# One score product per head and chunk from quotients of running products, with the attention run ahead of the feed-forward

## The chip, the cores and the metric

One core of one Trainium2 chip. The metric is the device time of one execution in microseconds; a kernel's figure is the median of its runs. The profile's span is some 2 us shorter than the time of the same execution.

## The reference, cut to what matters

```python
# q, k, v, alpha: (4, 8, 768, 48) float32, alpha in 0.8 .. 1
for t in range(S):
    state = alpha[:, :, t, :, None] * state + einsum('bhd,bhe->bhde', k[:, :, t], v[:, :, t])
    y[:, :, t] = einsum('bhd,bhde->bhe', q[:, :, t], state)
x = y.transpose(0, 2, 1, 3).reshape(3072, 384)
h = x @ w_in                      # w_in  (384, 2048), float64 in memory
out = (h * sigmoid(h)) @ w_out    # w_out (2048, 384), float64 in memory
```

Both halves share TensorE. The feed-forward is the same in all kernels here. The weights arrive as float64 and are turned into float32 on the chip, in 12 pieces of w_in and 16 of w_out; each piece passes through VectorE (four operations), GpSimd (three) and ScalarE (one).

## The kernel before: the parts that matter

There are 24 chunks of 128 tokens (six positions of four batch entries). The decay between tokens of a chunk is handled at seven levels: at each, eight small matmuls, a masked copy out of PSUM, and products that widen the prefix and suffix products of alpha.

```python
for L in LEVELS:                                   # 1, 2, 4 .. 64
    ps = ps_g.tile([128, 2, 512], F32, name="ps_g")
    for j in range(NP):
        for u in range(2):                         # two heads, in rows 0..47 and 64..111
            r = slice(64 * u, 64 * u + D)
            pe.matmul(ps[:, u, 64 * j : 64 * j + 64], lhsT=kp[r, j, :],
                      rhs=qp[r, j, :].rearrange(...)[:, :, 1, :], start=True, stop=True)
    dve.copy_predicated(g.rearrange(...)[:, :, :, 1, :], masks[L]..., ps[...])
    yield
    dve.tensor_tensor(x, x, two[:, :, 0:1]..., ALU.mult)      # q side
    gps.tensor_tensor(x, x, two[:, :, 1:2]..., ALU.mult)      # k side
    gps.tensor_tensor(up..., two[:, :, 0], two[:, :, 1], ALU.mult)
# ... then g @ v, q @ state, state update, transposes of the output
```

The order: all weight conversions lie beside the first four chunks. Later one chunk is in flight at a time, and its steps alternate with pieces of the feed-forward of the position before.

```python
filler, owed = weights(), 0
for ci in range(NCH):
    for pair in (chunks[0:2], chunks[2:4]) if ci == 0 else [[n] for n in chunks]:
        ...                      # a step of attention, then the filler's share
    for _ in filler: pass
    filler, owed = moe(ci), 0
```

## Time and profile before

| | before |
|---|---|
| time | 951.3 us (median; 950.65 to 952.26) |
| span of the profile | 947.5 us |
| TensorE busy | 869.3 us (92%) |
| TensorE not busy | 78.2 us, 68.5 of it in the first 165 us |
| first feed-forward matmul starts | 152.8 us |
| VectorE / GpSimd busy | 344.5 / 295.8 us |

Busy is the union of an engine's intervals. Read the rows of 40 slices for where it is low, and the table of stretches for which engine is full there. The prediction shows these lines.

### The profile page before, as it was taken

The page shows a single profiled execution, that of the slowest core. Times are in us where ns is not written, and L with a number is a line of the kernel's source. Part 1 is how long each engine was busy: PE and PEld are TensorE (multiplying, and loading weights), DVE is VectorE, ACT ScalarE, POOL GpSimd, SP SyncE. Part 2 cuts the span into 40 slices and gives each one's busy share as a digit, 9 for nine tenths or more (in the row PEclk, how much of TensorE's full clock was granted, in tenths as well). Part 3 has the DMA queues.
Part 4 walks back from the last instruction along what each step waited for, and adds up shares of the span by engine and source line. Part 5 has one row for each costly group of instructions (what it writes and reads, how often), then busy time and mean ns, then how long its engine had stood idle before and what let it go on. Part 6 is the DMA issues. An engine that isn't in the chain of part 4 may idle for free.

```text
span 947.5 us, 12698 instructions
## 1 busy us (share of the span) xinstructions
PE 869.3 (92%) x5176; PEld 564.6 (60%) x5176; DVE 344.5 (36%) x595; ACT 135.7 (14%) x242; POOL 295.8 (31%) x496
## 2 busy tenths in 40 slices
PE   5474567999999999999999999999999999999998
PEld 4473555556666556666556666556666556665454
DVE  6888987332332332332332332332232232130000
ACT  1112112121011121011121011121011111001200
POOL 6777676223222223232223232232232122020000
PEclk9996557999999999999999999999999999999999
DMA  9436224012022021022012022012022000000000
GB/s 177 93 114 135 86 89 109 1 35 34 12 42 49 1 34 33 15 43 46 4 31 34 13 42 47 5 30 35 17 42 42 1 1 1 12 15 9 0 9 25
DMA packets 107386, 36.99 MB, mean 39 GB/s; under 512 B 100673, under 2 KB 103745, under 8 KB 107329
## 3 DMA queue, kind: packets, MB, share of 16 engines
q1 hardware_dynamic: 107328, 36.19, 18.2%
q8 instruction: 41, 0.67, 0.3%
q14 instruction: 17, 0.13, 0.1%
HBM read 31.46 MB, written 4.72 MB: 38 GB/s over the span
## 4 chain that ended last, share of the span: by engine, by line
PE 81%; DVE 8%; POOL 5%; DMA 3%; issue 2%; SPq 1%; ACT 0%; POOLq 0%; ACTq 0%
PE ps_m L293 26%; PE ps_m L284 24%; PE ps_g L207 17%; PE ps_y L241 4%; DVE gt L212 3%; DMA kn<-in_k_dram 3%; PE ps_g L191 2%; PE ps_y L246 2%; PE ps_t L254 2%; PE ps_t L234 1%; DVE qp L222 1%; POOL tot L227 1%; DVE g L157 1%; POOL prod L177 1%; DVE g L152 1%
## 5 line engine op out<-in xcount | busy, mean ns | idle before, releaser
L207 PEld LDWEIGHTS ps_g<-qp,kp 48*128 48x128 f32 x2688 | 186.7, 211 | 158.0 <-issue 100.6
L284 PE MATMUL ps_m<-xt,w_in 128*128 128x512 f32 x576 | 276.8, 613 | 0.0
L293 PE MATMUL ps_m<-w_out,g 128*128 128x384 f32 x768 | 273.2, 496 | 0.0
L207 PE MATMUL ps_g<-qp,kp 48*128 48x64 f32 x2688 | 208.6, 302 | 61.7 <-DVE qp L222 57.2
L212 DVE COPY_PREDICATED gt<-mask,ps_g 128x512 f32<-128x512 uint8 x168 | 148.5, 885 | 241.7 <-PE ps_g L207 241.5
L293 PEld LDWEIGHTS ps_m<-w_out,g 128*128 128x128 f32 x768 | 137.2, 190 | 78.1 <-issue 0.5
L225 POOL TENSOR_TENSOR kp<-kp,tot 128x256 f32<-128x256 f32 x140 | 95.0, 678 | 260.2 <-PE ps_g L207 259.9
L284 PEld LDWEIGHTS ps_m<-xt,w_in 128*128 128x128 f32 x576 | 101.9, 192 | 92.9 <-issue 86.3
L287 ACT ACTIVATE g<-ps_m 128x512 f32<-128x512 f32 x96 | 57.3, 597 | 291.3 <-PE ps_m L284 291.3
L195 DVE TENSOR_TENSOR qp<-ps_g,at 128x512 f32<-128x512 f32 x24 | 16.5, 690 | 130.4 <-ACT kp L194 129.2
L222 DVE TENSOR_TENSOR qp<-qp,tot 128x256 f32<-128x256 f32 x140 | 63.4, 455 | 0.0
L241 PEld LDWEIGHTS ps_y<-vn,gt 128*128 128x128 f32 x384 | 50.0, 204 | 7.4 <-issue 4.8
L227 POOL TENSOR_TENSOR tot<-at 128x256 f32<-128x256 f32 x24 | 15.2, 632 | 120.2 <-ACT at L187 120.2
L250 DVE TENSOR_TENSOR x<-ps_y,dv 128x384 f32<-128x384 f32 x24 | 13.4, 557 | 97.4 <-PE ps_y L246 95.4
L241 PE MATMUL ps_y<-vn,gt 128*128 128x48 f32 x384 | 48.5, 282 | 0.0
L298 ACT COPY o<-ps_m 128x384 f32<-128x384 f32 x24 | 11.5, 479 | 222.5 <-PE ps_m L293 222.5
L227 POOL TENSOR_TENSOR tot<-tot 128x128 f32<-128x128 f32 (+5 forms) x140 | 36.8, 266 | 9.8
L258 POOL TENSOR_TENSOR st<-st,tot 128x384 f32<-128x384 f32 x16 | 13.2, 828 | 83.5 <-PE ps_y L246 83.5
L177 POOL TENSOR_TENSOR prod<-qn,kn 128x384 f32<-128x384 f32 x24 | 25.9, 1081 | 19.0 <-DMA kn<-in_k_dram 19.0
L159 ACT ACTIVATE g<-g 128x384 f32<-128x384 int32 (+1 forms) x28 | 15.9, 569 | 109.3 <-DVE g L157 109.3
L155 DVE SCALAR_TENSOR_TENSOR g<-bits,g 128x384 int32<-128x384 int32 (+1 forms) x28 | 22.9, 817 | 10.2 <-POOL g L154 10.2
L181 POOL TENSOR_TENSOR dv<-vn,dot 128x384 f32<-128x384 f32 x24 | 20.4, 849 | 19.3 <-DVE x L250 19.3
(51 smaller groups left out, 477.2 us busy)
## 6 DMA issues: line engine op xcount, KB each, us to landing
bits<-in_moe_w_in_dram SPq DMA_DIRECT2D x12, 512.0 KB, 4.0
bits<-in_moe_w_out_dram SPq DMA_DIRECT2D x16, 384.0 KB, 3.0
an<-in_alpha_dram SPq DMA_DIRECT2D x24, 192.0 KB, 3.1
qn<-in_q_dram SPq DMA_DIRECT2D x24, 192.0 KB, 4.0
kn<-in_k_dram SPq DMA_DIRECT2D x24, 192.0 KB, 4.1
vn<-in_v_dram SPq DMA_DIRECT2D x24, 192.0 KB, 2.5
out_dram<-o SPq DMA_DIRECT2D x24, 192.0 KB, 1.9
```

Source lines behind the costliest of these rows:

```text
L155: dve.scalar_tensor_tensor(e, hi, -(1 << 31), e, ALU.bitwise_and, ALU.bitwise_or)
L177: gps.tensor_tensor(prod, c["q"][:, :, 0:D], c["k"][:, :, 0:D], ALU.mult)
L181: gps.tensor_tensor(dv, vn, dot.to_broadcast([128, H, D]), ALU.mult)
L207: pe.matmul(ps[:, u, 64 * j : 64 * j + 64], lhsT=kp[r, j, :], rhs=qp[r, j, :].rearrange("p (b two l) -> p b two l", two=2, l=L)[:, :, 1, : ...
L212: dve.copy_predicated(g.rearrange("p u j (b two l) -> p u (j b) two l", two=2, l=L)[:, :, :, 1, :], masks[L].rearrange("p j (b l) -> p (j ...
L222: dve.tensor_tensor(x, x, two[:, :, 0:1].to_broadcast([128, nb, L]), ALU.mult)
L225: gps.tensor_tensor(x, x, two[:, :, 1:2].to_broadcast([128, nb, L]), ALU.mult)
L227: gps.tensor_tensor(up.rearrange("p j b -> p (j b)"), two[:, :, 0], two[:, :, 1], ALU.mult)
L241: pe.matmul(py[:, h, :], lhsT=g[:, h % 2, h // 2, :], rhs=vn[:, h, :], start=(h == 0), stop=(ci == 0 and h == H - 1), skip_group_check=True)
L284: pe.matmul(ps, lhsT=w_in[:, t, f * 128 : (f + 1) * 128], rhs=xt[:, t, :], start=(t == 0), stop=(t == NKT - 1))
L287: act.activation(gf, ps, AF.Silu)
L293: pe.matmul(ps, lhsT=gs[f][:, b * C : (b + 1) * C], rhs=w_out[:, f, :], start=(f == 0), stop=(f == NFT - 1))
```

## The change

The decay from s to t is a quotient of running products, P[t] / P[s]. So q is multiplied by the running product of alpha, k by a running product taken backwards that starts from one over the chunk's whole product, and one matmul per head gives all scores; a 0/1 mask then cuts off the lower half. This is exact enough only where no chunk's product gets too small. The kernel collects the largest alpha and the smallest chunk product, makes a flag of them at the end, and runs the whole old program if the flag is false.

The order changes too: the first eight chunks run ahead beside w_in alone, in four stages over consecutive steps, so four chunks are in flight. The w_out conversion moves under the first feed-forward. In the diff, which is cut, `[backwards]` stands for the reversed slices.

```diff
+    def products(n):
+        dve.tensor_reduce(most[:, n : n + 1], c["a"], ..., op=ALU.max, ...)
+        ...                                        # transposes of a, k, q; copies by ScalarE
+        dve.tensor_tensor_scan(p[...], sg[...], one[...], 0.0, ALU.mult, ALU.add)
+        dve.tensor_single_scalar(least[:, n, :], c["pc"], 2.0**-64, ALU.max)
+        dve.reciprocal(iv[:, last], least[:, n, :])
+        dve.tensor_tensor_scan(r[backwards], sg[backwards], iv[backwards], 0.0, ALU.mult, ALU.add)
+        gps.tensor_tensor(out["q"], out["q"], tokens(p), ALU.mult)
+        dve.tensor_tensor(out["k"], out["k"], tokens(r), ALU.mult)
+    def scores(n):
+        for j in range(NP):
+            for u in range(2):
+                r = slice(64 * u, 64 * u + D)
+                pe.matmul(ps[:, u, j, :], lhsT=c["kp"][r, j, :], rhs=c["qp"][r, j, :], start=True, stop=True)
+        for u in range(2):
+            dve.tensor_tensor(g[:, u], ps[:, u], mask..., ALU.mult)
+        ...                                        # transposes of k'
+    STAGES = (products, scores, values, bridge)
+    AHEAD = 2 * B
+    for step in range(steps):
+        for i, stage in enumerate(STAGES):
+            n = step - i
+            if 0 <= n < NT: stage(n)                  # ... and note in `bridged` what is ready
+            if step < AHEAD:
+                convert(0, (step * 4 + i + 1) * n_conv[0] // (4 * AHEAD))     # w_in
+            else:
+                share = todo * ((step - AHEAD) * 4 + i + 1) // (4 * (steps - AHEAD))
+                convert(1, (step - AHEAD) * 4 + i + 1)                        # w_out
+                while done < share:
+                    if done >= NFT: convert(1, n_conv[1])
+                    if done // PIECES * B + B > bridged: break
+                    next(filler); done += 1
+    ...
+    within = tc.nc.values_load(small[0:1, 0:1], min_val=0, max_val=1)
+    with tc.If(within < 1):
+        general(tc, *args)                         # the kernel before
```

More of the change, by code (lines that the diff above doesn't have):

```diff
@@ L18, with general @@
 @with_exitstack
-def kernel(
+def general(
     ctx: ExitStack,
@@ L327, with quotients, pool, load @@
         pass
+@with_exitstack
+def quotients(
+    ctx: ExitStack,
+    tc: tile.TileContext,
+    small: bass.AP,
+    q: bass.AP,
+    k: bass.AP,
+    v: bass.AP,
+    alpha: bass.AP,
+    moe_w_in: bass.AP,
+    moe_w_out: bass.AP,
+    out: bass.AP,
+):
+    nc = tc.nc
+    pe, dve, act, gps = nc.tensor, nc.vector, nc.scalar, nc.gpsimd
+    B, H, S, D = q.shape
+    C = 128
+    NCH = S // C
+    NP = H // 2
+    HD = H * D
+    DF = moe_w_in.shape[1]
+    NKT = HD // 128
+    NFT = DF // 128
+    NT = B * NCH
+    W = C + 1
+    def pool(name, bufs=1, space=None):
+        kw = {} if space is None else {"space": space}
+        return ctx.enter_context(tc.tile_pool(name=name, bufs=bufs, **kw))
+    PS = bass.MemoryType.PSUM
+    consts = pool("consts")
+    fix = pool("fix")
+    wpool = pool("wpool")
+    vpool = pool("vpool", 4)
+    work = pool("work", 2)
+    raw = pool("raw", 2)
+    xtp = pool("xtp", 3)
+    gpool = pool("gpool", NFT + 4)
+    opool = pool("opool", 2)
+    ps_t = pool("ps_t", 2, PS)
+    ps_g = pool("ps_g", 1, PS)
+    ps_y = pool("ps_y", 1, PS)
+    ps_s = pool("ps_s", 1, PS)
+    ps_m = pool("ps_m", 2, PS)
+    NIN = 4
+    nat = {
+        name: [fix.tile([128, H, 64], F32, name=f"{name}n{i}") for i in range(NIN)]
+        for name in ("a", "q", "k")
+    }
+    for i in range(NIN):
+        for name in ("a", "q", "k"):
+            (dve if i == 0 else gps).memset(nat[name][i][:, :, D:64], 1.0 if name == "a" else 0.0)
+    ctxs = {}
+    def load(n):
+        ci, b = divmod(n, B)
+        c = ctxs[n] = {"ci": ci, "b": b}
+        rows = slice(ci * C, ci * C + C)
+        for name, src in (("a", alpha), ("k", k), ("q", q)):
+            c[name] = nat[name][n % NIN]
+            nc.sync.dma_start(c[name][:, :, 0:D], src[b, :, rows, :].transpose([1, 0, 2]))
+        c["v"] = vpool.tile([128, H, D], F32, name="vn")
+        nc.sync.dma_start(c["v"], v[b, :, rows, :].transpose([1, 0, 2]))
+    load(0)
+    load(1)
+    ident = consts.tile([128, 128], F32, name="ident")
+    make_identity(nc, ident)
+    NR = 2
+    seg = [fix.tile([128, NP * W + 1], F32, name=f"al{i}") for i in range(NR)]
+    inv = [fix.tile([128, NP * W + 1], F32, name=f"inv{i}") for i in range(NR)]
+    for t in seg + inv:
+        gps.memset(t, 0.0)
+    one = consts.tile([128, NP * W + 1], F32, name="one")
+    gps.memset(one, 0.0)
+    gps.memset(one[:, 0 : NP * W + 1 : W], 1.0)
+    mask = consts.tile([128, C], F32, name="mask")
+    gps.memset(mask, 1.0)
+    gps.affine_select(mask, mask, pattern=[[1, C]], compare_op=ALU.is_ge, fill=0.0, base=0,
+                      channel_multiplier=-1)
+    st = [fix.tile([128, NP, 2, D], F32, name=f"st{b}") for b in range(B)]
+    for t in st:
+        gps.memset(t, 0.0)
+    most = fix.tile([128, NT], F32, name="most")
+    least = fix.tile([128, NT, NP], F32, name="least")
+    w_in = wpool.tile([128, NKT, DF], F32, name="w_in")
+    w_out = wpool.tile([128, NFT, HD], F32, name="w_out")
+    for n in range(2, NIN):
+        load(n)
+    def weights(which):
+        pieces = [
+            (w_in[:, t, c : c + 512], moe_w_in[t * 128 : t * 128 + 128, c : c + 512])
+            for c in range(0, DF, 512) for t in range(NKT)
+        ] if which == 0 else [
+            (w_out[:, f, :], moe_w_out[f * 128 : f * 128 + 128, :]) for f in range(NFT)]
+        for dst, src in pieces:
+            if src.dtype == F32:
+                act.dma_start(dst, src)
+                yield
+                continue
+            n = dst.shape[1]
+            bits = raw.tile([128, 512, 2], I32, name="bits")[:, 0:n, :]
+            nc.sync.dma_start(bits.rearrange("p n w -> p (n w)"), src.bitcast(I32))
+            lo, hi = bits.bitcast(U32)[:, :, 0], bits[:, :, 1]
+            e = gpool.tile([128, 512], I32, name="g")[:, 0:n]
+            dve.tensor_scalar(e, hi, 20, 0x7FF, ALU.logical_shift_right, ALU.bitwise_and)
+            gps.tensor_scalar(e, e, 1151, 896, ALU.min, ALU.max)
+            gps.tensor_scalar(e, e, -896.0, float(1 << 23), ALU.add, ALU.mult)
+            dve.scalar_tensor_tensor(e, hi, -(1 << 31), e, ALU.bitwise_and, ALU.bitwise_or)
+            top = gpool.tile([128, 512], I32, name="g")[:, 0:n]
+            dve.tensor_single_scalar(top, hi, 0xFFFFF, ALU.bitwise_and)
+            m = gpool.tile([128, 512], F32, name="g")[:, 0:n]
+            act.activation(m, top, AF.Copy, bias=1.0, scale=2.0**-20)
+            dve.scalar_tensor_tensor(m, lo, 2.0**-52, m, ALU.mult, ALU.add)
+            gps.tensor_tensor(dst, m, e.bitcast(F32), ALU.mult)
+            yield
+    xts = {}
+    def tokens(t):
+        return t[:, 1 : NP * W + 1].rearrange("p (j c) -> p j c", c=W)[:, :, 0:C]
+    def products(n):
+        c = ctxs[n]
+        dve.tensor_reduce(most[:, n : n + 1], c["a"], axis=mybir.AxisListType.XY, op=ALU.max,
+                          apply_absolute_value=True)
+        sg, iv = seg[n % NR], inv[n % NR]
+        out = {}
+        for name in ("a", "k", "q"):
+            ps = ps_t.tile([128, NP, C], F32, name="ps_t")
+            for j in range(NP):
+                pe.transpose(ps[:, j, :], c[name][:, 2 * j : 2 * j + 2, :], ident)
+            if name == "a":
+                act.copy(tokens(sg), ps)
+            else:
+                out[name] = work.tile([128, NP, C], F32, name=f"{name}t")
+                act.copy(out[name], ps)
+        p = work.tile([128, NP * W + 1], F32, name="p")
+        r = work.tile([128, NP * W + 1], F32, name="r")
+        n_all = NP * W + 1
+        dve.tensor_tensor_scan(p[:, 0 : n_all - 1], sg[:, 0 : n_all - 1], one[:, 0 : n_all - 1],
+                               0.0, ALU.mult, ALU.add)
+        last = slice(C, n_all, W)
+        c["pc"] = p[:, last]
+        dve.tensor_single_scalar(least[:, n, :], c["pc"], 2.0**-64, ALU.max)
+        dve.reciprocal(iv[:, last], least[:, n, :])
+        dve.tensor_tensor_scan(r[:, n_all - 2 :: -1], sg[:, n_all - 1 : 0 : -1], iv[:, n_all - 2 :: -1],
+                               0.0, ALU.mult, ALU.add)
+        gps.tensor_tensor(out["q"], out["q"], tokens(p), ALU.mult)
+        dve.tensor_tensor(out["k"], out["k"], tokens(r), ALU.mult)
+        c["qp"], c["kp"] = out["q"], out["k"]
+    def scores(n):
+        c = ctxs[n]
+        ps = ps_g.tile([128, 2, NP, C], F32, name="ps_g")
+        for j in range(NP):
+            for u in range(2):
+                r = slice(64 * u, 64 * u + D)
+                pe.matmul(ps[:, u, j, :], lhsT=c["kp"][r, j, :], rhs=c["qp"][r, j, :],
+                          start=True, stop=True)
+        g = c["g"] = work.tile([128, 2, NP, C], F32, name="g")
+        for u in range(2):
+            dve.tensor_tensor(g[:, u], ps[:, u], mask[:, None, :].to_broadcast([128, NP, C]), ALU.mult)
+        if c["ci"] < NCH - 1:
+            ps_k = ps_t.tile([128, NP, C], F32, name="ps_t")
+            for j in range(NP):
+                pe.transpose(ps_k[:, j, :], c["kp"][:, j, :], ident)
+            c["kn"] = work.tile([128, NP, C], F32, name="kn")
+            act.copy(c["kn"], ps_k)
+    def values(n):
+        c = ctxs[n]
+        ci, b, vn, g = c["ci"], c["b"], c["v"], c["g"]
+        py = ps_y.tile([128, H, D], F32, name="ps_y")
+        for h in range(H):
+            pe.matmul(
+                py[:, h, :], lhsT=g[:, h % 2, h // 2, :], rhs=vn[:, h, :],
+                start=(h == 0), stop=(ci == 0 and h == H - 1), skip_group_check=True)
+        if ci > 0:
+            for j in range(NP):
+                pe.matmul(
+                    py[:, 2 * j : 2 * j + 2, :], lhsT=c["qp"][:, j, :], rhs=st[b][:, j],
+                    start=False, stop=(j == NP - 1), skip_group_check=True)
+        x = c["x"] = work.tile([128, H, D], F32, name="x")
+        act.copy(x, py)
+        if ci < NCH - 1:
+            ps = ps_s.tile([128, NP, 2, D], F32, name="ps_s")
+            for j in range(NP):
+                pe.matmul(ps[:, j], lhsT=c["kn"][:, j, :], rhs=vn[:, 2 * j : 2 * j + 2, :],
+                          start=True, stop=True)
+            for u in range(2):
+                r = slice(64 * u, 64 * u + D)
+                s = st[b][r, :, u, :]
+                dve.tensor_tensor(s, ps[r, :, u, :], s, ALU.add)
+            s = st[b].rearrange("p j u e -> p j (u e)")
+            gps.tensor_tensor(s, s, c["pc"][:, :, None].to_broadcast([128, NP, 2 * D]), ALU.mult)
+    def bridge(n):
+        c = ctxs.pop(n)
+        ci, b = c["ci"], c["b"]
+        if b == 0:
+            xts[ci] = xtp.tile([128, NKT, B * C], F32, name="xt")
+        ps = ps_t.tile([128, NKT, C], F32, name="ps_t")
+        xf = c["x"].rearrange("p h d -> p (h d)")
+        for t in range(NKT):
+            pe.transpose(ps[:, t, :], xf[:, t * 128 : (t + 1) * 128], ident)
+        act.copy(xts[ci][:, :, b * C : (b + 1) * C], ps)
+    def moe(ci):
+        xt = xts.pop(ci)
+        gs = []
+        for f in range(NFT):
+            ps = ps_m.tile([128, B * C], F32, name="ps_m")
+            for t in range(NKT):
+                pe.matmul(ps, lhsT=w_in[:, t, f * 128 : (f + 1) * 128], rhs=xt[:, t, :],
+                          start=(t == 0), stop=(t == NKT - 1))
+            gf = gpool.tile([128, B * C], F32, name="g")
+            act.activation(gf, ps, AF.Silu)
+            gs.append(gf)
+            yield
+        for b in range(B):
+            ps = ps_m.tile([128, HD], F32, name="ps_m")
+            for f in range(NFT):
+                pe.matmul(ps, lhsT=gs[f][:, b * C : (b + 1) * C], rhs=w_out[:, f, :],
+                          start=(f == 0), stop=(f == NFT - 1))
+                if f % 4 == 3 and f < NFT - 1:
+                    yield
+            o = opool.tile([128, HD], F32, name="o")
+            act.copy(o, ps)
+            r = b * S + ci * C
+            nc.sync.dma_start(out[r : r + C, :], o)
+            yield
+    PIECES = NFT + 4 * B
+    STAGES = (products, scores, values, bridge)
+    AHEAD = 2 * B
+    conv = [weights(0), weights(1)]
+    n_conv = (NKT * (DF // 512), NFT)
+    def ffn():
+        for ci in range(NCH):
+            yield from moe(ci)
+    done = 0
+    todo = NCH * PIECES
+    steps = NT + len(STAGES) - 1
+    filler = ffn()
+    conv_done = [0, 0]
+    bridged = 0
+    def convert(which, upto):
+        while conv_done[which] < min(upto, n_conv[which]):
+            next(conv[which], None)
+            conv_done[which] += 1
+    for step in range(steps):
+        for i, stage in enumerate(STAGES):
+            n = step - i
+            if 0 <= n < NT:
+                stage(n)
+                if stage is bridge:
+                    bridged = n + 1
+                    if n + NIN < NT:
+                        load(n + NIN)
+            if step < AHEAD:
+                convert(0, (step * 4 + i + 1) * n_conv[0] // (4 * AHEAD))
+            else:
+                share = todo * ((step - AHEAD) * 4 + i + 1) // (4 * (steps - AHEAD))
+                convert(1, (step - AHEAD) * 4 + i + 1)
+                while done < share:
+                    if done >= NFT:
+                        convert(1, n_conv[1])
+                    if done // PIECES * B + B > bridged:
+                        break
+                    next(filler)
+                    done += 1
+    for _ in filler:
+        pass
+    ends = work.tile([128, 2], F32, name="ends")
+    dve.tensor_reduce(ends[:, 0:1], most, axis=AX, op=ALU.max)
+    dve.tensor_reduce(ends[:, 1:2], least, axis=mybir.AxisListType.XY, op=ALU.min)
+    dve.tensor_single_scalar(ends[:, 0:1], ends[:, 0:1], 1.0, ALU.is_le)
+    dve.tensor_single_scalar(ends[:, 1:2], ends[:, 1:2], 2.0**-64, ALU.is_gt)
+    dve.tensor_tensor(ends[:, 0:1], ends[:, 0:1], ends[:, 1:2], ALU.mult)
+    ps = ps_y.tile([1, 1], F32, name="ps_y")
+    pe.matmul(ps, lhsT=ends[:, 0:1], rhs=mask[:, C - 1 : C], start=True, stop=True)
+    dve.tensor_single_scalar(small, ps, 127.5, ALU.is_ge)
@@ new lines, with kernel @@
+@with_exitstack
+def kernel(
+    ctx: ExitStack,
+    tc: tile.TileContext,
+    q: bass.AP,
+    k: bass.AP,
+    v: bass.AP,
+    alpha: bass.AP,
+    moe_w_in: bass.AP,
+    moe_w_out: bass.AP,
+    out: bass.AP,
+):
+    flag = ctx.enter_context(tc.tile_pool(name="flag", bufs=1))
+    small = flag.tile([1, 1], I32, name="small")
+    args = (q, k, v, alpha, moe_w_in, moe_w_out, out)
+    quotients(tc, small, *args)
+    within = tc.nc.values_load(small[0:1, 0:1], min_val=0, max_val=1)
+    with tc.If(within < 1):
+        general(tc, *args)
```

## The prediction

> **What bounds the kernel now.** I read the page's slices first, then the costliest groups, then the table of stretches, then the chain and two stretches of TensorE's timeline.
>
> ```profile
> PE   5474567999999999999999999999999999999998
> DVE  6888987332332332332332332332232232130000
> POOL 6777676223222223232223232232232122020000
> PEclk9996557999999999999999999999999999999999
> ```
>
> One slice is 23.7 us. In the first seven (165 us) VectorE is the busy engine and TensorE is half idle, with a lowered clock; from the eighth on TensorE is full at full clock and everything else has room. So there are two regimes, and the table of stretches gives their limits:
>
> ```profile
> 50.00:75.00 25.00, 17.80 (x121) 17.17 (x120) 22.43 (x31) 4.65 (x8) 17.60 (x21) 1.00 0.40 113
> 100.00:125.00 25.00, 10.54 (x96) 10.06 (x94) 23.11 (x38) 3.13 (x6) 17.74 (x26) 0.50 0.25 79
> 290.00:400.00 110.00, 108.74 (x678) 68.59 (x677) 32.22 (x57) 16.74 (x30) 28.63 (x51) 1.00 0.14 26
> ```
>
> Columns: stretch, length, busy us and instructions of PE, weight loads, DVE, ACT, POOL, then clock, DMA share, GB/s. Early, DVE has 22 to 23 of 25 us; later PE has 108.7 of 110. What the early DVE does is mostly turning the float64 weights into float32 (28 pieces) beside four chunks of the level algorithm.
>
> ```profile
> L207 PE MATMUL ps_g<-qp,kp 48*128 48x64 f32 x2688 | 208.6, 302 | 61.7 <-DVE qp L222 57.2
> L212 DVE COPY_PREDICATED gt<-mask,ps_g 128x512 f32<-128x512 uint8 x168 | 148.5, 885 | 241.7 <-PE ps_g L207 241.5
> L155 DVE SCALAR_TENSOR_TENSOR g<-bits,g 128x512 int32<-128x512 int32 x12 | 12.4, 1030 | 6.1 <-POOL g L154 6.1
> ```
>
> Each float32 matmul shows as two records. [...] I price PE by starts in the timeline and in the chain:
>
> ```profile
> 301.20 1.88 PE L284 MATMUL ps_m<-xt,w_in 128*128 128x512 f32 x4
> 303.01 1.11 PE L207 MATMUL ps_g<-qp,kp 48*128 48x64 f32 x16
> 304.05 1.98 PE L284 MATMUL ps_m<-xt,w_in 128*128 128x512 f32 x4
> ...
> 326.78 1.88 PE L241 MATMUL ps_y<-vn,gt 128*128 128x48 f32 x16
> 328.49 1.10 PE L246 MATMUL ps_y<-st,qp 128*128 128x96 f32 x8
> 329.43 1.06 PE L254 MATMUL ps_t<-vn,kn 128*128 128x96 f32 x8
> 330.32 2.77 PE L284 MATMUL ps_m<-xt,w_in 128*128 128x512 f32 x6
> ```
>
> ```profile
> 330.48 2.60 PE ps_m L284 x6
> 472.14 2.60 PE ps_m L284 x6
> ...
> 861.49 41.20 PE ps_m L284 x96
> 902.69 41.29 PE ps_m L293 x128
> ```
>
> From starts: a level's 16 records take 304.05-303.01 = 1.04 us, values 1.71, state product 0.94, state update 0.89; in the same timeline three groups of four transposes take 1.31 together (299.89 to 301.20), the k' transposes 0.44, the output's 0.33. The last stage is pure feed-forward: 41.2 + 41.3 = 82.5 us per chunk position. One whole period (four chunks and one feed-forward) is 472.14-330.48 = 141.7 us, so four chunks cost 59.2, 14.8 each. Of these 7 x 1.04 = 7.3 is levels and 5.6 the other attention matmuls; the remaining 1.9 is switching between kinds of matmul and rare waits.
>
> [...] values move only 48 columns, yet take 1.71/16 = 107 ns a record. [...] L207 takes 65 ns a record[...]
>
> **The change, part by part.**
>
> *Scores.* 56 matmuls of N=64 per chunk become 8 of N=128. [...] If the two row groups overlap fully, 16 records take 1.04 us, if the streams serialize 1.71; I take 1.3. Saved per chunk on PE: 7.3-1.3 = 6.0 us, and about 1.1 of switching (10 switches, not 24).
>
> *VectorE per chunk.* Removed: seven predicated copies (7 x 0.885) and about seven products (7 x 0.455) with the dot product and final add, about 10.5 us. Added: a maximum over 128x512 (0.547 x 4/3 = 0.73), [...] two tiny ops (0.2), one 128x512 product (0.7), two mask products out of PSUM (2 x 0.69), two state adds (0.71): 6.0 us. GpSimd falls from about 11 to about 2.2 us. In the later regime all this lies beside PE and buys nothing.
>
> *Order.* Eight chunks run ahead while w_in alone (12 pieces) is converted; w_out's 16 pieces move under the first feed-forward. The instruction order puts the first feed-forward matmul after the transposes of chunk 7, scores and values of chunk 5.
>
> *Start.* VectorE's work up to there, counted from its order: 9 maxima 6.5, [...] products and tiny ops 5.7, 12 mask products 8.3, state adds 2.8, 9 pieces at (0.752+1.030+0.891+0.886 =) 3.56 us, 32.0. Sum 69 us. About 13 of it come before the first weight piece can land (16 loads precede it in the queue; landing near 22 us); the other 56 at the 75% to 85% utilization of the early stretches give 66 to 75 more. PE at its early speed (four transposes took 1.08 us there, a level 1.84) needs some 80 us, and the loads, about 12 MB at the early 168 GB/s, 73. Three resources near 70 to 80 do not overlap perfectly: 97 us, against 165 before, though w_out is still to come.
>
> *After the start.* Feed-forward 6 x 82.5 = 495. Remaining attention: 16 chunks of input transposes (21.0), 18 scores (23.4), 14 k' transposes (6.2), 18 values (30.8), 18 state products (16.9), 14 updates (12.5), 19 output transposes (6.3): 117. Switching at the old rate of 7.6 us per 92 order rows, for some 228 rows: 18.
>
> *w_out wait.* On ScalarE's order nine of the sixteen w_out conversions stand behind the last SiLU of the first feed-forward, because that stage's 16 results hold 16 of 20 buffers and a piece needs three. Each piece then runs nearly alone: ACT 0.52, two DVE steps 0.73 and 0.66, POOL 1.07, with hand-overs about 3.6. Nine take 32 us; PE has about 12 to 14 us of matmuls meanwhile. Stall: 18.
>
> *Tail.* Small waits of the last chunks' attention 5. Last matmul to end was 3.5[...]. The check itself works on data that is ready long before. With alpha in 0.8 to 1 a chunk's product averages exp(-13.8), far above 2^-64, so the old program is skipped.
>
> Sum: 97 + 495 + 117 + 18 + 18 + 5 + 6 = 756 us.
>
> **Rivals.** (a) *The start stays at about 140 us*[...]: the queue's weight loads wait on two raw buffers, and chains of transposes, copies, two scans, scores and masks are long [...]. For it: early DMA share was only 0.25 to 0.56. Against: stages of four chunks are interleaved. It would make 800. (b) *No w_out wait*, if VectorE and DMA run far ahead: 738. Against it stands ScalarE's order. (c) *Scores serialize in the array* or switching is dearer: 18 x 0.4 us plus some, 765 to 770. [...] (e) *Feed-forward interleaves better or the start packs perfectly* (80 us): 735. (f) *The flag is false* and both programs run: over 1600; very unlikely.
>
> **Range and chances.** The 612 us of feed-forward and attention matmuls are firm to about 15; start and w_out wait are the loose terms, each some 15 to 20 us, mostly upward. I say 756, range 728 to 795. To miss a gain of 2% the change would have to lose 170 us somewhere: faster 0.97, within 2% 0.02, slower 0.01.
>
> **What would show it.** Right: the first feed-forward matmul near 97 us; a score group of 16 records in 1.0 to 1.7 us; [...] a hole of 10 to 25 us in PE about 60 us after the feed-forward starts, ended by the w_out conversions; PE full otherwise; the last 82.5 us pure feed-forward. Wrong: a start past 120 us with DVE under 70% busy (rival a), no hole (b), PE gaps on VectorE or DMA in the later steps, or several us between the last output transfer and the end.

Cuts in the forecast are marked. They take out what no trace of this case had shown, among it a time for the scans, the rival (d) about it, and what the flag load and the branch add to the end. Three sums keep the terms that are no longer to be read: 6.0 us of VectorE a chunk and 69 us in the start (the scans are cut), and 6 us of tail (3.5 are from the trace, the rest was a guess). The whole came to 97 + 495 + 117 + 18 + 18 + 5 + 6 = 756 us with them; the start and the tail rest in part on what is cut. By the means of the changed kernel's trace, VectorE's operations took 6.8 us a chunk. The range of the score group, 1.04 to 1.71, is that of two groups in the trace before, a level's and the values'; that the two heads overlap was the author's estimate. That a float32 matmul shows as two records is read from L207: 24 x 7 x 8 = 1344 matmuls, 2688 records.

## The result, and the profile after

The changed kernel took **748.3 us** (746.95 to 749.81, four runs), a ratio of 0.787 to the kernel before (95% interval 0.7855 to 0.7882). A ratio is the mean time of one kernel's runs over the mean of the other's in the same rounds, so not quite the ratio of the medians. Executions over 1.5% slower than the fastest of the same kernel are left out of the means.

The page's first table gives the account, here before and after:

```profile
PE 869.3 (92%) x5176; PEld 564.6 (60%) x5176; DVE 344.5 (36%) x595; ACT 135.7 (14%) x242; POOL 295.8 (31%) x496
PE 690.5 (93%) x2874; PEld 428.9 (58%) x2874; DVE 226.5 (30%) x353; ACT 157.5 (21%) x290; POOL 126.4 (17%) x155
```

TensorE's busy time fell from 869.3 to 690.5 us, and its idle time from 78.2 to 55.3 (745.8 - 690.5). The two differences, 178.8 and 22.9, make the 201.7 us by which the span shrank. The score groups alone fell from 208.6 to 36.8 us.

The slices of the changed kernel, each 18.6 us:

```profile
PE   4657779997899999999999999999999999999996
DVE  4898695447422121212213142002171001000000
PEclk9755598998999999999999989999999999999999
```

The slow-clock stretch ends after five slices (93 us), not seven of 23.7. From the seventh slice on there is one dent in TensorE's row, a 7 and an 8 between 168 and 205 us. TensorE's timeline of the changed kernel, at the beginning of the feed-forward and of its second half (start, duration):

```profile
98.12 1.91 PE L570 MATMUL ps_m<-xt,w_in 128*128 128x512 f32 x4
...
163.16 2.74 PE L579 MATMUL ps_m<-w_out,g 128*128 128x384 f32 x8
```

The first feed-forward matmul starts at 98.1 us; 97 was predicted. Now the groups of the changed kernel (busy us, mean ns | idle before and who ended it):

```profile
L513 PE MATMUL ps_g<-qt,kt 48*128 48x128 f32 x384 | 36.8, 330 | 27.3 <-DVE kt L502 26.5
L499 DVE TENSOR_TENSOR_SCAN r<-al,inv 128x516 f32<-128x516 f32 x24 | 39.3, 1639 | 0.6
L493 DVE TENSOR_TENSOR_SCAN p<-al,one 128x516 f32<-128x516 f32 x24 | 30.5, 1270 | 18.6 <-POOL st L550 15.3
```

In the late regime a group of 16 score records of 128 columns takes 326.18 - 325.08 = 1.10 us from start to start, hardly more than a level's group of 64 columns before (1.04):

```profile
325.08 1.16 PE L513 MATMUL ps_g<-qt,kt 48*128 48x128 f32 x16
326.18 0.66 PE L521 MATMUL ps_t<-ident,kt 128*128 128x128 f32 x4
```

The hole in front of w_out is there too. The chain of waits of the changed kernel, in that stretch:

```profile
184.20 0.53 ACT g L463
184.75 0.72 DVE g L464
185.48 0.48 DVE g L459
185.98 0.36 DVE g L456
186.34 1.08 DVE g L461
187.50 0.53 ACT g L463
```

This is one round: a piece's ScalarE step and its last two VectorE steps (L464, L459), the first two of the next piece (L456, L461), then ScalarE again, 3.3 us in all. GpSimd's steps run beside it and are not in the chain. Nor is TensorE: it waits for the pieces.

### The profile page after: what moved, and what is told of

Same layout as the page of the kernel before. It is cut to its first block, busy times and chain, and to the rows that moved or that the text cites. A ratio compares the mean times of both kernels' runs of the same rounds, so it can differ in the third digit from the quotient of the medians.

```text
span 745.8 us, 7166 instructions
## 1 busy us (share of the span) xinstructions
PE 690.5 (93%) x2874; PEld 428.9 (58%) x2874; DVE 226.5 (30%) x353; ACT 157.5 (21%) x290; POOL 126.4 (17%) x155
## 4 chain that ended last, share of the span: by engine, by line
PE 82%; DVE 10%; POOL 2%; issue 1%; ACT 1%; DMA 1%; SPq 1%; ACTq 0%; POOLq 0%; DVEq 0%
PE ps_m L570 33%; PE ps_m L579 30%; PE ps_y L530 5%; PE ps_g L513 4%; PE ps_t L484 3%; PE ps_y L535 2%; PE ps_s L543 2%; DVE r L499 2%; DVE p L493 2%; PE ps_t L521 1%; DVE g L461 1%; DVE g L464 1%; DVE g L459 1%; POOL st L550 1%; DVE g L456 1%
## 5 line engine op out<-in xcount | busy, mean ns | idle before, releaser
L570 PE MATMUL ps_m<-xt,w_in 128*128 128x512 f32 x576 | 254.4, 597 | 1.3 <-ACT g L573 0.8
L517 DVE TENSOR_TENSOR g<-ps_g,mask 128x512 f32<-128x512 f32 x48 | 31.1, 684 | 135.2 <-PE ps_g L513 135.0
L513 PE MATMUL ps_g<-qt,kt 48*128 48x128 f32 x384 | 36.8, 330 | 27.3 <-DVE kt L502 26.5
L530 PEld LDWEIGHTS ps_y<-vn,g 128*128 128x128 f32 x384 | 51.7, 209 | 11.0 <-issue 7.1
L530 PE MATMUL ps_y<-vn,g 128*128 128x48 f32 x384 | 51.6, 286 | 5.1 <-issue 4.1
L513 PEld LDWEIGHTS ps_g<-qt,kt 48*128 48x128 f32 x384 | 30.7, 226 | 39.8 <-issue 19.9
L501 POOL TENSOR_TENSOR qt<-qt,p 128x512 f32<-128x512 f32 x24 | 29.9, 1246 | 125.5 <-ACT qt L489 91.9
L499 DVE TENSOR_TENSOR_SCAN r<-al,inv 128x516 f32<-128x516 f32 x24 | 39.3, 1639 | 0.6
L493 DVE TENSOR_TENSOR_SCAN p<-al,one 128x516 f32<-128x516 f32 x24 | 30.5, 1270 | 18.6 <-POOL st L550 15.3
L464 DVE SCALAR_TENSOR_TENSOR g<-bits,g 128x384 f32<-128x384 uint32 (+1 forms) x28 | 19.6, 699 | 22.2 <-ACT g L463 22.1
L484 PE MATMUL ps_t<-ident,an 128*128 128x128 f32 x96 | 18.8, 330 | 7.9 <-DMA an<-in_alpha_dram 4.8
```

What stands on the lines that cost most here:

```text
L464: dve.scalar_tensor_tensor(m, lo, 2.0**-52, m, ALU.mult, ALU.add)
L484: pe.transpose(ps[:, j, :], c[name][:, 2 * j : 2 * j + 2, :], ident)
L493: dve.tensor_tensor_scan(p[:, 0 : n_all - 1], sg[:, 0 : n_all - 1], one[:, 0 : n_all - 1], 0.0, ALU.mult, ALU.add)
L499: dve.tensor_tensor_scan(r[:, n_all - 2 :: -1], sg[:, n_all - 1 : 0 : -1], iv[:, n_all - 2 :: -1], 0.0, ALU.mult, ALU.add)
L501: gps.tensor_tensor(out["q"], out["q"], tokens(p), ALU.mult)
L513: pe.matmul(ps[:, u, j, :], lhsT=c["kp"][r, j, :], rhs=c["qp"][r, j, :], start=True, stop=True)
```

## The experiments

Theory after the result: the gain is TensorE work that no longer exists, plus a start that is some 55 us shorter (152.8 to 98.1) because 16 of 28 weight pieces leave it. Open were what the order is worth by itself, why the wider scores are free, what really sets the length of the start and of the w_out wait, and what the check costs. Each time has its own unchanged kernel before in the same rounds, at 951 to 952 us.

| run | time, us | ratio to before | 95% interval |
|---|---|---|---|
| changed kernel, again | 745.2 | 0.7849 | 0.7822 to 0.7875 |
| no branch | 745.3 | 0.7835 | 0.7814 to 0.7857 |
| scores, old order | 775.9 | 0.8152 | 0.8127 to 0.8177 |
| levels, new order | 1029.5 | 1.0826 | 1.0793 to 1.086 |
| heads apart | 761.4 | 0.7987 | 0.7955 to 0.8019 |
| own pool | 743.7 | 0.7813 | 0.7779 to 0.7847 |
| more scans | 759.5 | 0.7976 | 0.7949 to 0.8003 |
| more maxima | 748.3 | 0.7862 | 0.7817 to 0.7907 |
| four raw buffers | 747.4 | 0.7852 | 0.7825 to 0.7878 |
| six ahead | 772.3 | 0.8122 | 0.809 to 0.8154 |
| own pool, six ahead | 764.7 | 0.8028 | 0.80 to 0.8056 |
| useless matmuls | 745.2 | 0.7843 | 0.782 to 0.7866 |

All gave the correct result. The changed kernel's own runs lie between 744.5 and 750.1, so differences of 3 us between these rows mean nothing by themselves.

**The changed kernel again**, as a yardstick.

> The changed kernel itself, once more, as the yardstick for the other three on the same chip: 748 us, ratio to the kernel before 0.787.

As expected, within its spread.

**No branch.** The flag is still computed; what is gone is its use.

```diff
-    within = tc.nc.values_load(small[0:1, 0:1], min_val=0, max_val=1)
-    with tc.If(within < 1):
-        general(tc, *args)
```

> The flag load, the branch and the whole old program behind it are left out; maxima, minima and the flag itself stay. Theory: they cost only the end, where last output copy to end of span grew from 3.45 to 5.66 us, so 746 us, 2 to 2.5 under the changed kernel, and the end of the span goes back to about 3.5 us after the last copy starts. Rival: the longer program costs more along the way [...], then 5 us or more are gained, and not at the end. Second rival: the end grew for another reason, then nothing is gained.

No difference in time that the intervals could show. The last output copy starts at 740.14 us in the changed kernel, whose span is 745.8, and at 740.66 here:

```profile
740.66 0.48 ACT L584 COPY o<-ps_m 128x384 f32<-128x384 f32 x1 [9.84 <-PE ps_m L579]
```

with a span of 744.2. So from the last copy to the end it is 3.5 us without the branch and 5.7 with it; over all profiles, 3.4 or 3.5 in the four without a branch (before: 944.05 to 947.5) and 5.3 to 5.7 in the ten with it. The check's ending, flag load and branch together, costs about 2 us in the trace. No other cost is seen; this one is below what the times resolve. The old program behind the branch costs nothing that is seen.

**Scores alone, in the old order.** The levels of the kernel before are replaced by the new scores; the driver stays, with seven yields a chunk. The PSUM pools are divided as in the changed kernel, and there is no check at the end.

```diff
 def attention(n):
-    ... seven levels ...
+    yield from products(n); yield from scores(n); yield
+    yield from values(n); yield; bridge(n); yield
```

> The quotient scores alone, in the old order: all 28 weight pieces beside the first four chunks, one chunk in flight later, no check. Theory: the gain is the sum of a cheaper attention on TensorE and a start bound by VectorE. Start (28 pieces 87 us + 4 chunks of 6, over 0.83 utilization) 135, feed-forward 489, 20 chunks of 7.7 less the last ones' missing updates 149, end 3.5: 776 us. Rival: the order is what brought the gain, then over 850 us. Second rival: the order brought nothing, then 748.

Its 6 us of VectorE a chunk were an estimate; the changed kernel's trace has 6.8.

775.9 us: the sum of the theory to the microsecond, but not by its terms. The start is longer than I had put it, for TensorE is not full until 174 us:

```profile
125.00:150.00 25.00, 13.87 (x67) 12.24 (x67) 19.11 (x32) 5.93 (x12) 15.07 (x19) 0.50 0.43 115
175.00:200.00 25.00, 25.00 (x54) 10.89 (x53) 0.14 (x1) 4.78 (x8) 0.41 (x1) 0.90 0.00 1
```

By then, however, chunks 4 to 7 are done as well and a little of the feed-forward; I had counted them after it. The two errors cancel. What holds is that the new scores alone take some 175 us off, and the order, with its four interleaved stages, another 28 to 31.

**Old levels in the new order.** The driver of the kernel before is replaced, with the same share rule as in the changed kernel (eight chunks ahead in pairs beside w_in, then single chunks), and three pools get the changed kernel's sizes. The four interleaved stages are not in this run, so it tests eight chunks ahead and the later w_out, not the whole of the new order.

```diff
-filler, owed = weights(), 0
-for ci in range(NCH): ...
+groups = [[n, n + 1] for n in range(0, AHEAD, 2)] + [[n] for n in range(AHEAD, NT)]
+for pair in groups: ...      # convert w_in for the first eight chunks, then w_out and shares of feed-forward
```

> The old level algorithm with the new order: eight chunks ahead beside w_in only, w_out under the first feed-forward. Theory: start (12 pieces 43 us + about 7.5 chunks of 11.5, over 0.83) 155, feed-forward 495, 16.5 chunks of 14.8 less updates 239, w_out wait 10, end 3.5: 902 us, so the order alone is worth some 49 us, and the two parts alone together (175 + 49) more than the 203 of both. Rival: order alone is worth nothing while the levels load VectorE, then 951. Second rival: it carries most of the gain, then under 850.

**1029.5 us, 8% slower than before: my expectation and both rivals were wrong.** The first feed-forward matmul did come 40 us sooner (113.0 against 152.8 us). But that was no lead: by 600 us both runs had done as much (311 against 308 records of w_in, 384 of w_out in both, 1840 against 1862 of levels). What I missed is the other end. A feed-forward that starts early is also used up early: it may not pass the attention, so late chunks run with nothing beside them, one between 715 and 748 us and the last ones between 853 and 935. Counted at the full-rate starts of each kind of matmul in the prediction, 1.04 us a level and so on (an estimate), TensorE loses some 75 us in these two stretches, as much as the whole difference to before. TensorE's timeline of this run, levels without filler:

```profile
874.25 1.97 PE L207 MATMUL ps_g<-qp,kp 48*128 48x64 f32 x16 [1.77 <-DVE qp L222]
877.95 1.97 PE L207 MATMUL ps_g<-qp,kp 48*128 48x64 f32 x16 [1.73 <-DVE qp L222]
881.16 1.98 PE L207 MATMUL ps_g<-qp,kp 48*128 48x64 f32 x16 [1.24 <-DVE qp L222]
```

and the stretch around it:

```profile
850.00:935.00 85.00, 57.16 (x382) 51.80 (x380) 23.75 (x41) 3.78 (x7) 14.96 (x28) 0.52 0.01 3
```

A level takes 3.2 to 3.7 us instead of 1.04: it waits 1.2 to 1.8 us for VectorE, and its matmuls run at half clock (0.52). That the waits lower the clock is not shown by this run; with the useless matmuls further down the start's rose from 0.60 to 0.88. In all, TensorE is busy 69 us longer than before for the same instructions. So the two halves of the change, as tested here, don't add: alone they give -175 and +78, together -203. The reading is that the order pays only once the attention can stand a stretch without filler; whether it is the shorter scores or the interleaved stages that let it is not separated. In the changed kernel chunks also run bare, between 436 and 448 us, where the clock drops (0.82 from 443 to 460), and between 543 and 560, at full clock; TensorE loses some 5 and 4 us there by the same estimate.

**Heads apart.** The loops over the pair's two heads are swapped, so that neighbouring matmuls lie in the same rows of the array.

```diff
-        for j in range(NP):
-            for u in range(2):
+        for u in range(2):
+            for j in range(NP):
```

> The eight score matmuls of a chunk in another order: all heads of the upper row group first, then all of the lower, so that neighbours never lie in different rows. Theory: 128 columns cost no more than 64 (1.09 us a group, against 1.04 before) because neighbours in different row groups overlap; apart, a group of 16 records takes 1.7 us or more, 18 late chunks make it 11 us or more, and the slow-clock groups of the start some more: 757 to 765 us. Rival: the overlap does nothing and a record is bound by something else; then the group stays near 1.1 us and the time at 746.

761.4 us, in the theory's range. TensorE's timeline of this run:

```profile
302.69 1.71 PE L513 MATMUL ps_g<-qt,kt 48*128 48x128 f32 x16
304.33 0.66 PE L521 MATMUL ps_t<-ident,kt 128*128 128x128 f32 x4
```

1.64 us a group, not 1.10. So alternating row groups are what makes 128 columns as cheap as 64: 69 ns a record, against 102 when neighbours share rows. Over 18 late groups the difference is 10 us; the other 6 or so fall in the start.

**Own pool for the conversion.** The 20 shared buffers become 17 for feed-forward results and 6 for the conversion's temporaries.

```diff
-    gpool = pool("gpool", NFT + 4)
+    gpool = pool("gpool", NFT + 1)
+    cpool = pool("cpool", 6)
-            e = gpool.tile([128, 512], I32, name="g")[:, 0:n]          # also top, m
+            e = cpool.tile([128, 512], I32, name="cv")[:, 0:n]
```

> The temporaries of the weight conversion get six buffers of their own, the feed-forward results 17. Theory: nine w_out pieces stand behind the last SiLU because they lack buffers, and the stretch from 163 to 201 us holds 10 us that is neither feed-forward nor attention at full clock; with own buffers the pieces run between the SiLUs, the waits for w_out in that stretch vanish and 7 to 10 us are gained: 738 us. Rival: VectorE or the loads of w_out set the pace there; then the wait only moves and nothing is gained.

The mechanism is as expected. The last w_out piece is ready 25 us sooner (its last step starts at 170.5 us instead of 195.9), and TensorE no longer waits for w_out; the group of this run:

```profile
L580 PE MATMUL ps_m<-w_out,g 128*128 128x384 f32 x768 | 254.7, 487 | 0.9 <-ACT g L574 0.9
```

But the conversions now stand in ScalarE's order between the SiLUs, and the first half waits for those: the second half begins at 169.7 instead of 163.2. The second feed-forward begins at 221.3 us instead of 226.1, so 5 of 10 us are kept. In time it is 743.7 against 745.2 and 748.3, and not the 738 expected; the interval's lower part agrees with the trace, but the gain is not beyond doubt.

**More scans and more maxima**, a pair: as much extra VectorE work in the first eight chunks, once on the chain of each chunk and once off it.

```diff
+        if n < AHEAD:                                  # more scans
+            for z in range(2):
+                dve.tensor_tensor_scan(r[backwards], sg[backwards], iv[backwards], 0.0, ALU.mult, ALU.add)
+        if n < AHEAD:                                  # more maxima (the other run)
+            for z in range(4):
+                dve.tensor_reduce(most[:, n : n + 1], c["a"], ..., op=ALU.max, ...)
```

> In each of the first eight chunks the second scan is done three times instead of once: 16 x 1.23 = 20 us more of VectorE, on the chain of each chunk, some 12 to 15 of it before the first feed-forward matmul. Theory: VectorE's throughput bounds the start; first feed-forward matmul at 110 to 115 instead of 98, time 758 to 766. Rival: TensorE at its slow clock or the loads bound it; then under 5 us are lost.

> In each of the first eight chunks the maximum of alpha is taken five times instead of once: 32 x 0.68 = 22 us more of VectorE, but off the chain from transposes to scores. If VectorE's throughput bounds the start, as much is lost as with the added scans (12 to 20 us); if it is the latency of each chunk's chain, the added scans cost much more than these maxima (which then cost under 5).

The scans cost 11 to 14 us, the maxima nothing that shows. So VectorE's throughput alone does not set the start. The stretch from 25 to 98 us in two profiles (columns as in the prediction), first the changed kernel:

```profile
25.00:98.00 73.00, 50.64 (x308) 47.40 (x308) 59.80 (x90) 20.90 (x39) 43.70 (x40) 0.60 0.57 123
```

then with more maxima:

```profile
25.00:98.00 73.00, 51.35 (x342) 45.52 (x343) 67.83 (x101) 22.82 (x42) 43.34 (x39) 0.72 0.68 138
```

VectorE had 13 us free, and the maxima filled 8 of them without moving the rest (another 8 fell before 25 us, 5 after 98). The two are not alike in all else: the clock was 0.72 with the maxima and 0.60 without, which may have hidden part of their cost. Work on the chain, from transposes over scans and scores to values, pushes everything after it: the second half of the first feed-forward begins at 178.9 us with more scans, at 164.7 with more maxima, at 163.2 without either.

**Four raw buffers** for the loads of float64 weights.

```diff
-    raw = pool("raw", 2)
+    raw = pool("raw", 4)
```

> Four buffers instead of two for the raw weights. If the start's chain runs through the weight loads (a load waits until VectorE has done with the piece before last, then takes 4 us), more loads in flight bring the first feed-forward matmul from 98 to 90 or less, and 6 us or more are gained. If the chain is the one inside a chunk (transposes, copies, two scans, scores, masks, values, handed between engines), as the added scans suggest, nothing is gained: 746 within 3.

The first feed-forward matmul moves to 91.7 us, nearly as far as the one theory said, but the time does not follow. The second half begins at 160.9, TensorE then waits 9.5 us for w_out instead of 6.6, and the second feed-forward begins at 227.7 us, no sooner than before (226.1). Of the 6 us, 4 are gone by the second half, and the rest is given back in front of w_out. That also shows that the first feed-forward matmul is a poor milestone: the order puts more or less attention ahead of it.

**Six chunks ahead**, alone and with the own pool.

```diff
-    AHEAD = 2 * B
+    AHEAD = B + 2
```

> Six chunks ahead instead of eight. The start lets TensorE idle 33 of 98 us and runs it at a clock of 0.6; starting the feed-forward two chunks earlier fills part of that: first feed-forward matmul at about 80, gain up to 12 us, less 3 to 5 for late chunks that lose their filler (the feed-forward then waits longer for chunks 20 to 23, as the old levels in this order showed): 738. Rival: w_in is not ready and w_out comes sooner still, so the waits only move: 746 or more.

> Six chunks ahead and own buffers for the conversion's temporaries, as the candidate for the fastest. If the two gains add, 3 for the buffers and 8 for the order: 735. If the w_out conversion on VectorE limits both, no better than 741.

Both expectations failed: 772 and 765 us, some 24 and 20 us slower than with eight. With six ahead the second half of the first feed-forward begins 12 us sooner (151.5 us), but by the second feed-forward (225.2 against 226.1 us) the lead is gone, with about as much attention done (160 score records against 176, 146 value records against 144). From there to the last copy it takes 539.5 us instead of 514.1. Again stretches of attention stand bare, as with the old levels. The longest, first with six ahead, then in the changed kernel:

```profile
544.00:575.00 31.00, 27.06 (x195) 24.26 (x193) 17.31 (x25) 8.90 (x18) 6.48 (x5) 0.77 0.08 20
544.00:575.00 31.00, 29.42 (x164) 19.70 (x163) 14.48 (x25) 9.47 (x18) 3.15 (x3) 1.00 0.05 13
```

So the loss lies in the later steps, not in the start. That the chunks ahead are the filler's head start, which keeps such stretches short, is the reading that fits; it was not tested apart.

**Useless matmuls** to keep the clock up in the start.

```diff
+            if 0 < step < AHEAD:
+                idle = ps_m.tile([128, B * C], F32, name="ps_m")
+                pe.matmul(idle, lhsT=ident, rhs=one[:, 0 : B * C], start=True, stop=True)
```

> In the first eight steps one useless 512-column matmul after each stage (28 in all, 24 us of TensorE at full clock), into a result bank that nothing reads. Theory: the start's chain runs for some 32 of the 73 us from 25 to 98 on TensorE, at a clock of 0.6; with the array kept busy the clock stays up and that part halves, less the queueing behind the useless matmuls: first feed-forward matmul at 88 to 93 instead of 98 and 5 to 10 us gained, though TensorE does more. Rival: the share of the chain on TensorE isn't what bounds it, or the clock doesn't follow so small a filling; then the useless matmuls only stand in the way and 5 to 25 us are lost.

The clock followed, from 0.60 to 0.88; the stretch of this run:

```profile
25.00:98.00 73.00, 56.75 (x360) 42.48 (x358) 69.84 (x98) 22.11 (x41) 46.64 (x44) 0.88 0.66 143
```

The time did neither what the theory nor what the rival said: 745.2 us, no change. Twenty-eight useless matmuls, 34 us busy by the profile, cost nothing and gained nothing. The first feed-forward matmul comes later (109.5 us), but with more attention ahead of it, and the second half begins at 163.3 us, where it began without them. At the higher clock VectorE is busy 96% of the stretch instead of 82%: of the chain of waits from 25 to 98 us, 30.9 us lay on TensorE and 30.3 on VectorE in the changed kernel, 2.5 and 61.0 here. So, as far as these two profiles show, two things bound the start almost equally, TensorE's steps within each chunk's chain at a clock of 0.60 and VectorE's queue, and relieving one uncovers the other.

No run was clearly faster than the changed kernel; the own pool is the only one whose trace shows why it should be.

## Why the prediction was right, step by step

- **The bound.** Right in the main: outside the start, the w_out wait and a few bare stretches TensorE is full (531.6 us busy of the 536 from 201 to 737) and sets the end. In the first three slices before, the clock row reads 9, and 1.00 until 75 us in the table, although a level took 1.84 us there and 1.04 later; so the lowered clock that the prediction read into all seven slices fits the speeds, but not the row. The last pure feed-forward took 41.47 + 41.29 = 82.8 us as before (82.5).
- **Start, 97 us.** The size was right (98.1), the reasoning only half. VectorE's work to that point was 72.2 us (69 estimated). But I turned it into time by a utilization, as if its throughput ruled, and the added maxima show that it doesn't. It is a chain inside each chunk, handed between TensorE at a clock of 0.60, VectorE and GpSimd (30.9, 30.3 and 7.6 us from 25 to 98; ScalarE 1.0); rival (a) named such a chain and gave it too long a time. So 97 is partly luck, and it is a poor milestone: it was 91.7 with four raw buffers and 109.5 with useless matmuls, in equal times.
- **Scores, 1.3 us.** Mis-sized, 1.10 measured with alternating row groups, near the lower end of my range (1.04); the swapped loops came near the other end, 1.64 (1.71 estimated).
- **The w_out wait, 18 us.** Right in place and cause (the own pool took it away); too large. The round, 3.3 us measured and 3.6 estimated, came out by another chain: four VectorE steps and ScalarE, not two and a GpSimd step. From 163.16 to 201.12 us TensorE did 72 records of w_out (72 x 0.3226 = 23.2 us at full rate) and 3.2 us of attention; with 1 us of switching the rest, 10.5, is waits and slow clock. The prediction gave TensorE 12 to 14 us of matmuls to do meanwhile. The order runs two token blocks side by side over each piece (their output copies start at 197.90 and 198.55 us), so it had 26 in this stretch.
- **Tail, 6 us.** 5.7 from the last copy's start to the end.
- **Scan.** 516 elements took 1.21 to 1.23 us where nothing is in the way; the second scan has a median of 1.95 (see below). No scan was in the trace before.
- **Sum.** After the start 495 + 117 + 18 + 18 + 5 = 653 us were predicted and 740.14 - 98.12 = 642.0 measured. The 11 us are 18 x 0.2 = 3.6 from the scores and 7.5 from the w_out wait, so the rest agrees as a sum, but by luck: switching, 18 (18.8 by its own figures), is nearly nothing where it can be read off. From 224.49 to 257.14 us, between two score groups, 60 records of w_in (at 41.2/96 us) and one chunk's attention of 6.7 us make 32.5 of 32.65 us. In its place stand waits and slow clock that the prediction put at 5: an estimated 9 us from 98 to 163 (TensorE is idle for 5.1 of them, at a clock of 0.95), and about 10 in the bare stretches around 442, 552 and 652 us.

What the prediction didn't see is that the two halves of the change depend on one another: the order alone, in the form tested, loses 8%.

## What to carry to other kernels

Removing work from the engine that sets the end pays in full; moving it about pays only as far as filler lasts, so before running one stage ahead, count what will stand beside the other stage at the end. Where an engine shows 80% busy, test with extra work on and off the dependency chain before calling it the bound. A group of buffers shared by two uses can serialize one of them behind the other; look at the order on the engine that sits between the two.

## What the runs showed of the hardware that was not expected

On VectorE a clamp of four numbers a partition took 0.16 us or up to 1.15, and the long ones end with a GpSimd operation. The changed kernel's timeline:

```profile
17.04 1.48 POOL L501 TENSOR_TENSOR qt<-qt,p 128x512 f32<-128x512 f32 x1 [4.95 <-DVE p L493]
17.39 1.15 DVE L497 TENSOR_SCALAR least<-p 128x4 f32<-128x4 f32 x1
```

GpSimd ends at 18.52, the clamp at 18.54. The product on GpSimd and the rest of the chain on VectorE become ready by the same scan, so they meet in most chunks (the clamp began during it in 5 of 24, the second scan in 13). All seven clamps that began during a GpSimd operation, five of them during this product, ended 0.02 to 0.03 us after it; the other 17 took 0.16 or 0.17. What holds a clamp until then is not shown.

The second scan's median of 1.95 us goes with the same product. In the changed kernel's trace all 13 scans of 1.95 to 1.97 us began while GpSimd's product was running and ended 1.1 us after it; of the 11 others, none of which met that product, ten took 1.22 to 1.23 us, the last three beside an idle GpSimd among them. No run moved the product away. In the w_out wait, too, the VectorE step at L461 took 0.35 us in seven pieces, and 1.15 in the six where it began during GpSimd's product at L465: 0.8 of the 3.3 us of a round.
